# Query blocks in order 0, 1, 3, 2, dense blocks' activations ahead of the one-hot rows, and weight halves formed a pair ahead

## Chip, cores and metric

The kernel runs on one core of a Trainium2 chip. The metric is the device time of one execution in microseconds, as a median over runs. The engines of the core each run their own list of instructions in order: TensorE (PE, matmuls), VectorE (DVE), ScalarE (ACT), GpSimd (POOL) and SyncE (SP, which here issues most transfers). They wait for one another by semaphores.

## What is computed

A layer norm of x (2048 tokens of width 512) feeds two branches, and the output is x plus both:

```python
# attention: 32 heads of 16, one shared key and value head
scores = einsum("bhqd,bkd->bhqk", xn @ wq, xn @ wk) * 16 ** -0.5
att    = (softmax(scores) @ (xn @ wv)) @ wo
...
# product-key experts: 8 chunks of 4 heads, 64 x 64 = 4096 experts
s1, s2 = q1 @ k1.T, q2 @ k2.T                  # 64 scores each, per token and head
# the two best of each, the two best of their four sums, softmax g over these two
act = gelu(einsum("nd,nhkd->nhk", xn, u[top_e]))
out = einsum("nhk,nhk,nhkd->nd", g, act, v[top_e])
```

The inputs are float32. Each token picks 32 heads times 2 experts = 64 rows of u and of v.

## The kernel before, in words

**Attention.** The queries stand in four blocks of 512 tokens. A unit is one query block and four heads, 32 units in all, listed in `units` (L293). Each unit passes over 16 key tiles, two of them to a step, so the main loop has 256 steps `d`, with `i = 2 * d` (`att_steps`, L1040). A step issues 4 score matmuls (`scores`, L318), 16 matmuls of the previous step's probabilities with the values (`pv`, L332), and 4 more score matmuls; ACT takes the exponentials (L321, four of 128 x 1024 to a step). When two units are done, their sums and rows go through DRAM (`pair_*`, L363 to L382) to the normalised `on` tiles. Four `on` tiles are one query block, which is then multiplied with `wo` in four groups of 4 matmuls (`block_out`, L423, output `pwo`). `wo` lies in two of the 12 tiles of 512 KB that the gathers use also (`load_wo`, L387; `lent`).

**Experts by gathers.** Token groups 0 and 1 (8 tiles of 128 tokens) fetch their rows: a slot is one tile, head and choice pair of 128 experts, 512 slots in all. POOL starts an indirect DMA of 512 KB (`g`, L883), DVE forms the dot with xn (L895), four slots together pass small operations and a tanh on ACT (L904 to L918), and DVE adds the weighted rows to the tile's total `xa` (L930). A new gather may start when there is a free tile: the order is fixed as the gather of slot m + 12 after the add of slot m (m + 10 while `lent` is 2; `gathers`, L937).

**Experts as dense products.** Token groups 2 and 3 multiply with all 4096 experts in 32 blocks of 128 (`dense`, L648). Before this, the indices and gates of the group's 32 heads, held in `da` tiles (L631 to L641), are transposed on PE (`ptd`, L714) and spread: for each 16 tokens, 32 times (`q` loop, L744), DVE compares with a table of positions `io` (L725, L727), multiplies the gates in (L728), and PE multiplies the two one-hot operands of each token (`pg`, L752, 32 columns wide) to a 128 x 32 table of gates. ACT copies it (L757), and it goes to DRAM (`dg`) and comes back by block (`gy<-dg`, `fetch_gates`). Then for each block b, L791 to L861: load the u and v rows (`rw`, `fetch`), split each into a rounded half and the rest (`split`: ACT L687, DVE L688, into `wk` tiles), 12 matmuls with the group's xn (`pact`, L799), the gelu chain on ACT and DVE (`gy`, L821 to L828), a split of its result (`wd`, L835), and for each two blocks 24 matmuls to the four token tiles (`pout`, L783), each group added to the tile's total on DVE (`da`, L786).

**What sets the order.** Inside `tc.manual_schedule` nothing is reordered: each engine runs what the text issues, in that order. Each step takes the attention work and then `fill()` lets `score_thread` (L1001) run ahead to a linear target of estimated cost, so PE's fill is evenly laid over the steps: first the scores of group 0's 8 chunks, two chunks of group 1, then group 2 with its dense part, six chunks of group 1, then group 3 with its dense part. DVE's slot work goes by a rate `pos` per step (L1155: 2.1 slots, later 1.7, 2.5 in the one-hot rows or 1.4 in the blocks, by `dense_on`), and from step 192 on what is left is laid evenly over the remaining steps. `mid()` issues the DVE work in the middle of a step; `behind`, `store`, `on_act`, `LATER`, `LAST` and `LATER_ACT` put single operations off to the next step's DVE, SP or ACT part. `flush()` issues them at once.

**Sums of the branches.** For query blocks 0 to 2 the two branches meet through DRAM: whichever is done first is stored to `d_part`, and the other loads it (`fin`, one buffer), adds and stores the output (`load_fin` L418, `block_out`, `experts_out` L446). `att_steps` issues the `pwo` groups of a block in every second step from `i % 128 == 16` on. The DVE addition of the attention part to a loaded `fin` is L433, that of the experts' part L452. Block 3 is added straight to its experts' total by `last_out_a` and `last_out_b` (L396, L402).

Of the kernel before, what the change touches and what calls it, by code (L numbers as in the profile page):

```python
# [23 lines left out]
P = 128  # L24
S = 2048
D = 512
# [22 lines left out]
C_CUB = 0.044715 * C_IN  # L49
MOST = 4.0  # L50
# [4 lines left out]
def tile_kernel(ctx, tc, x, wq, wkv, wo, wqT, kT, uv, ub, vb, out):  # L55
# [17 lines left out]
    d_w = [dram.tile([P, KC, 2, 512], F32, name=f"dw{c}") for c in range(NC)]  # L73
    d_g = dram.tile([NB, P, 512], F32, name="dg")
# [218 lines left out]
    units = [(qb, hg) for qb in range(4) for hg in range(8)]  # L293
# [43 lines left out]
    def unit_tail(u):  # L337
# [4 lines left out]
        def spread():  # L342
            if half == 0:
                ot = late[0].tile([P, 512], F32, name="ot", tag="ot", bufs=1)
                OT[pp] = ot
                if pp == 15:
                    rs = late[0].tile([P, 512], F32, name="rsb", tag="on", bufs=4)
                    RB[pp] = rs
# [29 lines left out]
    def pair_tail(pp):  # L378
        rs = RB.pop(pp)
        on = late[0].tile([P, 512], F32, name="on", tag="on", bufs=4)  # L380
        nc.vector.tensor_mul(on, OT.pop(pp), rs)
        ON[pp] = on  # L382

    DONE_A, DONE_B, OUTS = {}, {}, []
# [17 lines left out]
    def last_out_b():  # L402
# [6 lines left out]
        for j in range(4):  # L409
            t = 12 + j  # L410
            nc.vector.tensor_add(ACC[t], ACC[t], PL[j])
            (nc.sync, nc.scalar)[j % 2].dma_start(out[t * P:(t + 1) * P, :], ACC[t])
# [3 lines left out]
    FIN = {}  # L416

    def load_fin(t):  # L418
        fin = late[0].tile([P, D], F32, name="fin", tag="fin", bufs=1)
        nc.sync.dma_start(fin, d_part[t])  # L420
        FIN[t] = fin

    def block_out(qb, j):  # L423
        t = 4 * qb + j
        p = xtile("pwo")
        for k in range(KC):
            nc.tensor.matmul(p, ON[4 * qb + k][:, j * P:(j + 1) * P], WO[k // 2][:, k % 2, :],  # L427
                             start=k == 0, stop=k == KC - 1)
        if t in FIN:
            fin = FIN.pop(t)  # L430

            def total():
                nc.vector.tensor_add(fin, fin, p)  # L433
                store(lambda: nc.sync.dma_start(out[t * P:(t + 1) * P, :], fin))

            behind(total)
        else:
            def keep():
                fin = late[0].tile([P, D], F32, name="fin", tag="fin", bufs=1)
                nc.scalar.copy(fin, p)  # L440
                store(lambda: nc.sync.dma_start(d_part[t], fin))

            on_act(keep)
        DONE_A[t] = True

    def experts_out(t):  # L446

        if t >= 12:
            return True
        if t in FIN:  # L450
            fin = FIN.pop(t)
            nc.vector.tensor_add(fin, fin, ACC[t])  # L452
            store(lambda: nc.sync.dma_start(out[t * P:(t + 1) * P, :], fin))
        elif t in DONE_A:
            load_fin(t)
            return False
        else:
            acc = ACC[t]
            store(lambda: nc.sync.dma_start(d_part[t], acc))
        DONE_B[t] = True  # L460
        return True
# [94 lines left out]
    DT = []  # L556
# [7 lines left out]
    def batch(ph, c, b):  # L564
# [52 lines left out]
        if c == 0:  # L617
            DT.clear()
            dense_tiles()
# [14 lines left out]
        def gates():  # L634
# [8 lines left out]
            stt(dgt[:, :, 1, w], gg, GS, gh, op0=OP.mult, op1=OP.subtract)  # L643

# [3 lines left out]
    def dense(DG, after):  # L648

        df1, df2, dgt = DT[:3]  # L650
# [12 lines left out]
        def gate_tile(b):  # L663
            if b not in gates:
                gy = late[0].tile([P, 2, 512], F32, name="gy", tag="gy", bufs=3)
                gates[b] = gy
            return gates[b]

        def fetch_gates(b):
            if b < NB and b not in fetched:  # L670
                if formed[0] < b - 2:
# [3 lines left out]
                nc.sync.dma_start(gate_tile(b)[:, 0, :], d_g[b])  # L675
                fetched.add(b)

        splits, halved = {}, set()

        def split(b):  # L680
            if b < NB:
                if b not in raws:
                    run(STORES)
                rw = raws.pop(b)
                us, vs = wk_tile(), wk_tile()
                for i, w in enumerate((us, vs)):
                    nc.scalar.copy(w[:, 0, :], rw[:, i, :])  # L687
                    behind(lambda w=w, i=i: nc.vector.tensor_tensor(out=w[:, 1, :], in0=rw[:, i, :], in1=w[:, 0, :],  # L688
                                                                    op=OP.subtract))
                behind(lambda: halved.add(b))  # L690
                splits[b] = us, vs
# [11 lines left out]
        io = kt(F16, (P, P, TB))  # L703
# [4 lines left out]
        tr = kt(F16, (P, 3, 512))  # L708
        for n, src in enumerate((df1, df2, dgt)):
            if n == 2:  # L710
                yield None
            p = xtile("ptd")
            for j in range(GT):
                nc.tensor.transpose(p[:, j * P:(j + 1) * P], src[:, j].rearrange("p r s -> p (r s)"), ident)  # L714
            nc.scalar.copy(tr[:, n, :], p)
            yield 0.45
        dense_on[0] = 2
# [3 lines left out]
        def onehot(q):  # L721
            if q < NQ:
# [3 lines left out]
                ob = kt(F16, (P, NB, TB))  # L726
# [4 lines left out]
        def first_gates():  # L731

            fetch_gates(0)
            fetch_gates(1)
            for j in range(2):
                da = big.tile([P, 2, D], F32, name="da", tag="da", bufs=2)
                for i in range(2):
                    t = GT * DG + 2 * j + i
                    nc.sync.dma_start(da[:, i, :], x[t * P:(t + 1) * P, :])
                    ACC[t] = da[:, i, :]  # L740

        onehot(0)
        onehot(1)
        for q in range(NQ):  # L744
# [10 lines left out]
            def copies(pv_=pv_, st=st, ql=ql, t0=t0):  # L755
                for hb in range(2):
                    nc.scalar.copy(st[hb][:, :, ql * TB:(ql + 1) * TB], pv_[:, 16 * hb:16 * hb + 16, :])  # L757
                if ql == 3:
                    for hb in range(2):
                        store(lambda hb=hb: nc.sync.dma_start(  # L760
# [501 lines left out]
```

## Time and profile before

| | |
|---|---|
| median of 3 runs | 1995.04 us (1994.63, 1995.04, 2007.21) |
| the profiled execution, its own time | 2001.03 us |
| its span in the trace | 1999.3 us |
| PE busy | 1882.9 us, 94% |
| DVE busy | 1682.7 us, 84% |
| ACT busy | 1292.0 us, 65% |
| POOL busy | 570.8 us, 29% |
| DMA | 494.79 MB, 247 GB/s on average |

How to read it: a row of the windows view gives one stretch of the span, from and to in microseconds, its length, the busy time and number of instructions of each engine, the granted clock of PE as a share of full speed, and the busy share of the DMA engines. A row of the waits view gives engine and line that waited, what it waited for, the sum, how often, and the longest. A row of the timeline gives start, busy time, engine, line and what the instruction writes and reads; where the engine stood idle ahead of it, the idle time and its releaser stand in brackets. Busy times of neighbouring instructions on one engine overlap a little, so the price of one is the distance between two starts.

### The profile page before, as it was taken

How to read it: one execution, taken by the hardware profiler on the slowest of the kernel's cores; microseconds unless marked ns; L12 is line 12 of the kernel's file. 1: busy time of each engine (PE TensorE's matmuls, PEld its weight loads, DVE VectorE, ACT ScalarE, POOL GpSimd, SP SyncE). 2: the span in 40 equal slices, each digit the busy share in tenths (PEclk: the TensorE clock that was granted, in tenths of full speed). 3: DMA queues.
4: the chain of work that ended last, by engine and by line, in shares of the span. 5: the costliest groups of instructions: out<-in, count | busy, mean ns of one | idle time of the engine just before them, and what ended most of it. 6: DMA issues, size and time to landing. Idle time of an engine off the chain costs nothing.

```text
span 1999.3 us, 34729 instructions
## 1 busy us (share of the span) xinstructions
PE 1882.9 (94%) x10990; PEld 997.5 (50%) x10990; DVE 1682.7 (84%) x6713; ACT 1292.0 (65%) x1804; POOL 570.8 (29%) x542
## 2 busy tenths in 40 slices
PE   6869999999998998999999999999899789999997
PEld 4534444555554444555555455555445345555552
DVE  7537888999998786999999779999999668999993
ACT  3236666655556785787877565555568567788873
POOL 2202232222222232333444222222223333333320
PEclk9989999999997998999999999999979899999999
DMA  7847878977664878888889877777568877888762
GB/s 272 301 185 235 276 272 272 331 275 248 218 212 140 229 221 271 264 269 269 284 297 328 286 253 261 268 238 225 176 169 234 276 245 263 268 277 257 263 211 63
DMA packets 239882, 494.79 MB, mean 247 GB/s; under 512 B 93380, under 2 KB 93380, under 8 KB 239692
## 3 DMA queue, kind: packets, MB, share of 16 engines
q0 software_dynamic: 73728, 268.47, 40.5%
q1 hardware_dynamic: 163960, 222.44, 34.0%
q10 hardware_dynamic: 2004, 1.61, 0.3%
q8 instruction: 88, 1.44, 0.3%
q14 instruction: 102, 0.84, 0.1%
HBM read 429.51 MB, written 57.64 MB: 244 GB/s over the span
## 4 chain that ended last, share of the span: by engine, by line
PE 63%; DVE 20%; DMA 5%; issue 2%; ACT 2%; SPq 1%; DVEq 0%; ACTq 0%
PE pv L332 18%; PE sc L318 12%; PE psc L532 10%; PE pout L783 8%; PE pact L799 8%; DVE i L547 5%; DVE xa L930 4%; DVE m L545 3%; DVE g L895 3%; PE pg L752 3%; PE pw L487 2%; PE pwo L427 1%; DMA dg<-gst 1%; ACT pt L321 1%; DMA fin<-dpart 1%
## 5 line engine op out<-in xcount | busy, mean ns | idle before, releaser
L321 ACT ACTIVATE pt<-sc 128x1024 f32<-128x1024 f32 x1024 | 993.0, 1025 | 471.1 <-PE sc L318 424.6
L883 POOL DMA_INDIRECT g<-in_uv_dram,idx x512 | 554.0, 1082 | 1358.4 <-DVE xa L930 697.4
L332 PE MATMUL pv<-pt,vaug 128*32 128x512 f32 x4096 | 524.1, 631 | 0.0
L318 PE MATMUL sc<-qa,kaug 64*128 64x512 f32 x2048 | 389.1, 454 | 14.4 <-ACT pt L321 13.5
L532 PE MATMUL psc<-wk,xt 128*128 128x512 f32 x1536 | 388.2, 400 | 5.3 <-DMA xt<-dxt 3.2
L930 DVE SCALAR_TENSOR_TENSOR xa<-g,w,xa 128x512 f32<-128x512 f32 x512 | 370.6, 745 | 0.0
L895 DVE CUSTOM_DVE_ANT_0 g<-g,xa 128x512 f32<-128x512 f32 x512 | 336.1, 681 | 3.0 <-DMA g<-in_uv_dram,idx 3.0
L532 PEld LDWEIGHTS psc<-wk,xt 128*128 128x128 f32 x1536 | 277.8, 188 | 108.7 <-issue 38.5
L318 PEld LDWEIGHTS sc<-qa,kaug 64*128 64x128 f32 x2048 | 157.6, 187 | 338.2 <-ACT pt L321 203.5
L332 PEld LDWEIGHTS pv<-pt,vaug 128*32 128x32 f32 x4096 | 110.7, 113 | 263.4 <-issue 261.7
L799 PE MATMUL pact<-xt,wk 128*128 128x512 f32 x768 | 198.7, 404 | 14.6 <-DVE fin L433 6.3
L547 DVE FIND_INDEX8 i<-m,psc 128x8 uint32<-128x64 f32 x1024 | 206.4, 221 | 0.0
L783 PE MATMUL pout<-wk,wd 128*128 128x512 f32 x768 | 195.7, 402 | 8.7 <-DVE wd L835 4.7
L799 PEld LDWEIGHTS pact<-xt,wk 128*128 128x128 f32 x768 | 141.1, 190 | 65.4 <-issue 17.7
L783 PEld LDWEIGHTS pout<-wk,wd 128*128 128x128 f32 x768 | 140.6, 188 | 56.7 <-DVE wd L835 6.0
L545 DVE MAX8 m<-psc 128x8 f32<-128x64 f32 x1024 | 146.0, 214 | 22.2 <-PE psc L532 19.8
L786 DVE TENSOR_TENSOR da<-da,pout 128x512 f32<-128x512 f32 x128 | 82.7, 679 | 8.2 <-PE pout L783 7.9
L918 DVE SCALAR_TENSOR_TENSOR w<-gth,ga 128x4 f32<-128x4 f32 x128 | 20.2, 158 | 79.9 <-ACT gth L911 79.4
L688 DVE TENSOR_TENSOR wk<-rw,wk 128x512 fp32r<-128x512 f32 x128 | 84.8, 682 | 0.1
L725 DVE TENSOR_TENSOR oh<-oh 128x2048 f16<-128x2048 f16 x64 | 78.0, 1219 | 7.1 <-PE pg L752 7.1
L752 PE MATMUL pg<-oh 128*128 128x32 f16 x1024 | 73.4, 246 | 8.1 <-DVE oh L728 8.1
L687 ACT CAST wk<-rw 128x512 fp32r<-128x512 f32 x128 | 73.6, 628 | 9.0 <-DMA rw<-in_ub_dram 6.7
(150 smaller groups left out, 1341.8 us busy)
## 6 DMA issues: line engine op xcount, KB each, us to landing
wk<-dw SPq DMA_DIRECT2D x96, 512.0 KB
wqt<-in_wqT_dram SPq DMA_DIRECT2D x32, 512.0 KB
dw<-wk SPq DMA_DIRECT2D x32, 512.0 KB
rw<-in_ub_dram SPq DMA_DIRECT2D x64, 256.0 KB
rw<-in_vb_dram SPq DMA_DIRECT2D x64, 256.0 KB
dg<-gst SPq DMA_DIRECT2D x32, 512.0 KB
gy<-dg SPq DMA_DIRECT2D x64, 256.0 KB
qa<-dqh SPq DMA_DIRECT2D x128, 64.0 KB
```

Of the source, the lines that this page charges most:

```text
L318: nc.tensor.matmul(p[:, b, :], kaug[o:o + 64, kc * P:(kc + 1) * P], QA[u][o:o + 64, i, :], start=True, stop=True)
L321: nc.scalar.activation(pt, p, AF.Exp, scale=SCALE)
L332: nc.tensor.matmul(PV[u][32 * j:32 * j + 32, :], vaug[:, kc, :], pt[:, b, :], start=kc == 0, stop=kc == 15)
L532: nc.tensor.matmul(p, XT[g][k][:, a, j * P:(j + 1) * P], WC[n_][k][:, bb, :], start=n == 0, stop=n == 11)
L545: nc.vector.max(m8[:, jb, s, :], p[:, s * E:(s + 1) * E])
L547: nc.vector.max_index(i8[:, jb, s, :], m8[:, jb, s, :], p[:, s * E:(s + 1) * E])
L752: nc.tensor.matmul(p[:, i * NB:(i + 1) * NB], oa[:, :, i], ob[:, :, i], start=True, stop=True)
L783: nc.tensor.matmul(p, wd[:, a, j * P:(j + 1) * P], vs[:, c, :], start=n == 0, stop=n == 5)
L799: nc.tensor.matmul(p, us[:, a, k * P:(k + 1) * P], XT[DG][k][:, c, :], start=n == 0, stop=n == 11)
L883: nc.gpsimd.indirect_dma_start(out=gt, out_offset=None, in_=uv, in_offset=bass.IndirectOffsetOnAxis(ap=IDX[ph, c, ti][:, s:s + 1], axis=0))
L895: nc.vector.tensor_tensor_reduce(u, u, XN[TPH * ph + ti], scale=1.0, scalar=0.0, op0=OP.mult, op1=OP.add, accum_out=a[:, i:i + 1])
L930: nc.vector.scalar_tensor_tensor(acc, v, w[:, i:i + 1], acc, op0=OP.mult, op1=OP.add)
```

## The change

1. **Order of blocks.** The units go through query blocks 0, 1, 3, 2 (`QB`). Block 2 is now the last, whose attention meets the experts' totals at the end; its totals, finished by then, are stored to `d_part` and loaded back as `FT` three steps before the end of attention (`load_last`).
2. **Sums.** `fin`, `load_fin` and the additions through it are gone. `block_out` adds each `pwo` group by one DVE operation to the token tile's total itself (`xa` or `da`), which must be loaded by then (`LIVE`). `experts_out` only stores. The groups of block 0 and block 3 are issued between dense blocks 2, 3 and 4, or from `i % 128 >= 56` on, those of block 1 every second step as before. `wo` stays in its two gather tiles until `i % 128 == 64` (before: 30), but for `256 < i < 384`.
3. **First blocks early.** The dense generator starts ahead of the last chunk's four tiles: it loads the u and v rows of blocks 0 and 1 and splits the u halves while that chunk is scored. The 12 `pact` matmuls of block 0 and its chain up to (tanh + 1) times the product (`first(0)`) are issued ahead of the first transposes, those of block 1 after the first one-hot row. Only the multiplication by the gates is left for later. The table `io` comes by DMA from `d_io`, written in the prologue by one ACT copy and one store, in place of a POOL copy.
4. **Splits ahead.** The splits of blocks 0 to 3 are issued during the last eight of the 32 one-hot rows (before: of 0 and 1, in the last two rows, of 2 and 3 with the first blocks), the u halves of 2 and 3 ahead of their v halves. The three small one-hot operands lie in a ring of one tile. The last `gst` tile is stored in three parts: gates of blocks 0 to 2 first, then 3 to 15, then 16 to 31. The totals of the group (`da`) are loaded at block 2.
5. **Slots.** From the last but one one-hot row until block 4, and from the last chunk's third tile until the transposes are done (`dense_on` 3), the slot rate is 0 (before: 1.4 or 1.7) and at most one addition is issued in a step. Dots are no longer asked for beyond the gathers that were issued.
6. The `on` tiles have 5 buffers (before 4).

Both programs have 11928 PE and 7263 DVE instructions; ACT has 3 fewer, POOL 2 fewer and SP 11 fewer (1215 for 1226).

The diff, cut to its core:

```diff
+    d_io = dram.tile([P, P, 16], F16, name="dio")
...
+        io = gtile(F16, (P, P, 16))
+        nc.scalar.copy(io, iota_h[:, :, None].to_broadcast([P, P, 16]))
+        nc.sync.dma_start(d_io, io)
...
-    units = [(qb, hg) for qb in range(4) for hg in range(8)]
+    QB = (0, 1, 3, 2)
+    units = [(qb, hg) for qb in QB for hg in range(8)]
...
+    def block_out():
+        m, j = PWO.pop(0)
+        t = GT * QB[m] + j
...
-        if t in FIN:
...
+        acc = ACC[t]
+        behind(lambda: nc.vector.tensor_add(acc, acc, p))
...
+        store(lambda: nc.sync.dma_start(d_part[t] if last else out[t * P:(t + 1) * P, :], acc))
...
     def dense(DG, after):
...
+        def half_split(b, i):
+            rw, w = raws[b], wk_tile()
+            nc.scalar.copy(w[:, 0, :], rw[:, i, :])
+            behind(lambda: nc.vector.tensor_tensor(out=w[:, 1, :], in0=rw[:, i, :], in1=w[:, 0, :], op=OP.subtract))
+            return w
...
-        nc.gpsimd.tensor_copy(io, iota_h[:, :, None].to_broadcast([P, P, TB]))
+
         fetch(0)
         fetch(1)
-        yield None
...
+        yield 0.0
+        early = []
+        on_act(lambda: early.extend(half_split(b, 0) for b in range(2)))
+        yield 0.0
...
+        def first(b):
+            p = xtile("pact")
+            for k in activations(b, early[b], p):
+                if k < KC - 1:
+                    yield 3 * UNIT
+            g, y = gate_rows(b), hh[:, b, :]
+            nc.scalar.activation(y, p, AF.Square, scale=C_CUB ** 0.5)
+            nc.scalar.copy(g, p)
+            nc.vector.scalar_tensor_tensor(y, y, C_IN, p, op0=OP.add, op1=OP.mult)
+
+            def go():
+                nc.scalar.activation(y, y, AF.Tanh)
+                behind(lambda: nc.vector.scalar_tensor_tensor(y, y, 1.0, g, op0=OP.add, op1=OP.mult))
...
+        nc.sync.dma_start(io, d_io)
...
+        yield from first(0)
+        for n in range(2):
+            spread(n)
             yield 0.45
+        while not gated_all:
+            yield None
+        spread(2)
+        yield 0.45
...
+        obs = kt(F16, (P, 3, NB, TB))
         onehot(0)
+        yield from first(1)
         onehot(1)
         for q in range(NQ):
...
-            if q >= NQ - 2:
-                dense_on[0] = 1
-                later_split(q - NQ + 2)
+            if q in (NQ - 8, NQ - 5):
+                later_split((NQ - 8, NQ - 5).index(q))
+            if q == NQ - 3:
+                on_act(lambda: halves.__setitem__(2, half_split(2, 0)))
+            if q == NQ - 2:
+                dense_on[0] = 3
+                on_act(lambda: halves.__setitem__(3, half_split(3, 0)))
+                later_split(2)
+            if q == NQ - 1:
+                later_split(3)
...
+            def scaled(y=y, g=g):
+                multiplied[0] += 1
+                stt(g, g, 1.0 / GS, y, op0=OP.mult, op1=OP.mult)
...
+            if b == 4:
+                dense_on[0] = 1
+            if b in (2, 3) and out_ready():
+                block_out()
+                yield 3.6
...
     def score_thread():
...
+            if ph >= NSP and c == NC - 1:
+                dn = dense(ph, n + 1 if n + 1 < len(SEQ) else None)
+                yield next(dn)
             for ti in range(TPH):
+                if dn and ti == 1:
+                    yield next(dn)
+                if dn and ti == 2:
+                    dense_on[0] = 3
...
     def att_steps(d, mid, fill):
...
-        if out_now:
-            block_out(qb, j)
+        if out_ready() and (i % 128 >= HOLD and PWO[0][0] != 1 or i % 4 == 0 and PWO[0][0] == 1):
+            block_out()
             spent[0] += 3.6
...
+        if i == STEPS - 6:
+            load_last()
-        if i >= 128 and i % 128 == 30:
+        if i >= 128 and i % 128 == (30 if 256 < i < 384 else HOLD + 8):
             lent[0] = 0
...
-                pos += 2.1 if len(IDX) < NC * TPH else (1.7, 2.5, 1.4)[dense_on[0]]
+                pos += 2.1 if len(IDX) < NC * TPH else (1.7, 2.5, 1.4, 0.0)[dense_on[0]]
             else:
-                pos += max(0.0, NSL - pos) / max(half - 4 - d, 1)
+                pos += max(0.0, NSL - pos) / max(half - 4 - d, 1) if dense_on[0] < 3 else 0.0
...
+                if dense_on[0] == 3:
+                    sums = min(sums, 1)
```

More of the change, by code (lines that the diff above doesn't have):

```diff
@@ L423, in block_out @@
-    def block_out(qb, j):
-        t = 4 * qb + j
+    LIVE = set(range(GT))
+    PWO = []
+    def block_out():
+        m, j = PWO.pop(0)
+        t = GT * QB[m] + j
         p = xtile("pwo")
         for k in range(KC):
-            nc.tensor.matmul(p, ON[4 * qb + k][:, j * P:(j + 1) * P], WO[k // 2][:, k % 2, :],
+            nc.tensor.matmul(p, ON[4 * m + k][:, j * P:(j + 1) * P], WO[k // 2][:, k % 2, :],
                              start=k == 0, stop=k == KC - 1)
-        if t in FIN:
[L430 to L443, printed above, removed]
+        assert t in LIVE
+        acc = ACC[t]
+        behind(lambda: nc.vector.tensor_add(acc, acc, p))
@@ L444, in block_out, with out_ready @@
         DONE_A[t] = True
+    def out_ready():
+        return PWO and GT * QB[PWO[0][0]] + PWO[0][1] in LIVE
     def experts_out(t):
[L448 to L459, printed above, removed]
@@ L683, in split @@
                     run(STORES)
[L684 to L689, printed above, removed]
+                us = None if b < 2 else halves.pop(b) if b in halves else half_split(b, 0)
+                splits[b] = us, half_split(b, 1)
                 behind(lambda: halved.add(b))
-                splits[b] = us, vs
+                raws.pop(b)
         def later_split(b):
@@ L1013, in score_thread @@
             if ph >= NSP and c == NC - 1:
[L1014 removed]
+                yield from dn
                 dense_on[0] = 0
```

214 lines of the change are left out of this document (120 added, 94 removed).

## The prediction

> **What bounds the kernel now.** I read the page first, for the bound and the chain, then the windows view over the stretches around the two dense groups, then the waits inside them, then the timeline for prices.
>
> ```profile
> span 1999.3 us, 34729 instructions
> PE 1882.9 (94%) x10990; PEld 997.5 (50%) x10990; DVE 1682.7 (84%) x6713; ACT 1292.0 (65%) x1804; POOL 570.8 (29%) x542
> ...
> PE 63%; DVE 20%; DMA 5%; issue 2%; ACT 2%; SPq 1%; DVEq 0%; ACTq 0%
> ```
>
> PE is busy for 94% of the span and carries 63% of the chain; DVE is second with 84% and 20%. Both programs have the same number of PE and of DVE instructions, so a gain must come from time in which PE stands, or runs on a lowered clock, and a loss from places where DVE has more to do than PE. The rows of the stretches:
>
> ```profile
> core 0: us, PE busy (x) PEld busy (x) DVE busy (x) ACT busy (x) POOL busy (x), PEclk, DMA share, GB/s
> 597.00:621.00 24.00, 16.49 (x118) 7.26 (x116) 23.34 (x119) 14.31 (x20) 8.36 (x7) 0.90 0.56 178
> 621.00:657.20 36.20, 36.20 (x285) 17.24 (x283) 30.56 (x64) 24.79 (x42) 5.88 (x5) 0.74 0.41 125
> 657.20:741.50 84.30, 83.37 (x692) 41.81 (x690) 64.19 (x135) 68.50 (x110) 23.75 (x21) 0.98 0.84 227
> 741.50:800.00 58.50, 47.10 (x234) 22.24 (x238) 40.68 (x95) 36.96 (x54) 18.26 (x18) 0.85 0.83 271
> 1439.00:1463.50 24.50, 12.93 (x95) 6.81 (x94) 23.85 (x127) 10.24 (x15) 4.24 (x4) 0.78 0.40 140
> 1463.50:1558.00 94.50, 91.79 (x825) 47.91 (x824) 88.59 (x186) 75.27 (x127) 26.67 (x22) 0.88 0.78 209
> 1558.00:1648.00 90.00, 75.42 (x369) 33.45 (x367) 57.68 (x139) 53.04 (x76) 30.63 (x27) 0.89 0.82 268
> 1648.00:1960.00 312.00, 310.36 (x1758) 170.63 (x1760) 282.22 (x646) 244.11 (x346) 106.25 (x96) 1.00 0.76 247
> ```
>
> I call lost PE time the idle time plus the busy time times what the clock lacks. First group: index work and transposes (597 to 621) 24.00 - 16.49 + 16.49 x 0.10 = 9.2 us; one-hot rows (621 to 741.5) 36.20 x 0.26 + 0.93 + 83.37 x 0.02 = 12.0; first blocks (741.5 to 800) 11.4 + 47.10 x 0.15 = 18.5. Second group: 11.6 + 12.93 x 0.22 = 14.4; 2.7 + 91.79 x 0.12 = 13.7; 14.6 + 75.42 x 0.11 = 22.9. Together 90.7 us. The last row is the tail, the second group's blocks: PE loses 1.6 us in 312, while DVE is idle for 29.8. What PE waits for in those places:
>
> ```profile
> PE ptd L714 <- DVE da L631: 9.4, 2, 8.7
> PE pg L752 <- DVE oh L728: 8.1, 6, 2.7
> ...
> PE pact L799 <- DVE fin L433: 6.3, 1, 6.3
> ...
> PE pact L799 <- ACT wk L687: 5.0, 1, 5.0
> ```
>
> These are of the whole span. Inside 741.5 to 791, and then inside 1558 to 1648:
>
> ```profile
> PE pact L799 <- DVE wk L688: 3.3, 1, 3.3
> ...
> ACT wk L687 <- DMA rw<-in_ub_dram: 6.7, 1, 6.7
> ```
>
> ```profile
> PE pout L783 <- DVE fin L433: 3.6, 1, 3.6
> ...
> PE pwo L427 <- DVE fin L433: 1.4, 1, 1.4
> ...
> DVE fin L433 <- DMA fin<-dpart: 25.3, 3, 12.9
> ```
>
> So four things stop PE: DVE's index work ahead of the transposes, DVE's one-hot operands, splits that wait for late u and v rows, and, after the second group's one-hot rows, DVE standing 25.3 us behind three loads of `fin`.
>
> Prices of DVE work, by the distance of starts:
>
> ```profile
> 1700.29 0.68 DVE L825 SCALAR_TENSOR_TENSOR gy<-gy,pact 128x512 f32<-128x512 f32 x1
> 1700.89 0.68 DVE L895 CUSTOM_DVE_ANT_0 g<-g,xa 128x512 f32<-128x512 f32 x1
> ...
> 1701.50 0.68 DVE L895 CUSTOM_DVE_ANT_0 g<-g,xa 128x512 f32<-128x512 f32 x1
> ...
> 1703.45 1.40 DVE L930 SCALAR_TENSOR_TENSOR xa<-g,w,xa 128x512 f32<-128x512 f32 x2
> 1704.78 0.68 DVE L822 SCALAR_TENSOR_TENSOR gy<-gy,pact 128x512 f32<-128x512 f32 x1
> ```
>
> ```profile
> 1481.81 0.16 DVE L906 TENSOR_TENSOR ga<-act,gg 128x4 f32<-128x4 f32 x1
> 1481.89 1.22 DVE L725 TENSOR_TENSOR oh<-oh 128x2048 f16<-128x2048 f16 x1
> ...
> 1483.81 1.22 DVE L725 TENSOR_TENSOR oh<-oh 128x2048 f16<-128x2048 f16 x1
> ```
>
> A 512-wide operation takes 0.60, a dot 0.61, an addition 0.67 (two in 1.33), a small one 0.08; with four small ones to four slots a slot takes 1.35 us. A one-hot row takes 1.92.
>
> **The change, part by part.** The places of the work are counted in the written order of both programs, by attention step.
>
> *A. First transition and one-hot rows.* 24 `pact` matmuls (blocks 0 and 1) now stand among the transposes. By the first of the page's rows below, 198.7 / 768 = 0.26 us each, they are 6.2 us that PE has to do where it waited.
>
> ```profile
> L799 PE MATMUL pact<-xt,wk 128*128 128x512 f32 x768 | 198.7, 404 | 14.6 <-DVE fin L433 6.3
> L783 PE MATMUL pout<-wk,wd 128*128 128x512 f32 x768 | 195.7, 402 | 8.7 <-DVE wd L835 4.7
> ```
>
> Also 8 dots and 7 additions (10 us of DVE) that stood among the index work are issued later. I take 7 us off the 9.2. In the one-hot rows up to step 82 the change takes 16 `pwo` matmuls out of PE and adds five u and v subtractions (3.0 us) to DVE; both then have about 88 to 91 us of work over sixteen steps, so DVE still holds PE at times: 2 us off the 12.0. Ends: 0 and -21.2. A = -9.
>
> *B. First blocks.* The waits for `wk` (5.0, 3.3) and for the u rows (6.7 on ACT) end in splits of blocks 0 and 1 that are asked for in the last two rows. Issued eight and five rows before the end, at about 6 us a row, they have 30 us for a load. Late next is the gates' store and load (`dg`, `gy`), covered by block 2's 12 matmuls and the block-0 output groups placed there. -16 of 18.5; ends -18.5 and, if those gates come as late as the rows did, -8.
>
> *C. Second transition.* The same 6.2 us of matmuls stand against 11.6 idle. But only one `pg` group instead of two comes before the next attention step, and DVE has its backlog of slots behind it: -4; ends 0 and -11.6.
>
> *D. Second one-hot rows.* DVE gets more in the sixteen steps after the transposes: 35 dots for 31, 34 additions for 29, two one-hot rows more, in all 9.8 us by the prices above; 89 of 94.5 us were already busy. 5.9 us are slack, of which I count 2.3 as usable (the rest ended in waits on tanh that stay): +7.5. By the written order two dots there stand only 3.1 and 3.8 us of DVE work behind the addition that lets their gather start:
>
> ```profile
> 1563.70 1.56 POOL L883 DMA_INDIRECT g<-in_uv_dram,idx  x1 [0.30 <-issue]
> 1565.57 1.05 POOL L883 DMA_INDIRECT g<-in_uv_dram,idx  x1 [0.31 <-issue]
> ```
>
> ```profile
> 1569.48 0.70 DVE L895 CUSTOM_DVE_ANT_0 g<-g,xa 128x512 f32<-128x512 f32 x1 [0.53 <-DMA g<-in_uv_dram,idx]
> ...
> 1571.63 0.69 DVE L895 CUSTOM_DVE_ANT_0 g<-g,xa 128x512 f32<-128x512 f32 x1 [1.44 <-DMA g<-in_uv_dram,idx]
> ```
>
> Gathers issued at 1563.70 and 1565.57 held the dots of 1569.48 and 1571.63: 5.8 and 6.1 us from start to use. Two such waits: +2.5. D = +10; ends +4 and +16.
>
> *E. `fin`.* Without the loads DVE no longer stands 25.3 us, and PE's 6.3, 3.6 and 1.4 go, with the low clock behind them: -19 of 22.9; ends -15 and -22.9 (the rate 0 leaves DVE with 20 us of work there against PE's 47, so nothing else can hold PE but `wd`).
>
> *F. The tail.* What DVE doesn't do in the blocks' start it does later: the last 44 steps of attention (from step 208) hold 141 dots and 138 additions, before 103 and 103. 38 dots, 35 additions, ten groups of small operations more, two `fin` additions and four subtractions fewer and six `gy` operations more make +44 us by the prices above. DVE was busy 282.2 of 312 us; with 326 it passes PE's 310, which stays as it is (30 matmuls of `pact` and `pout` fewer, 8 of `pwo` more, 3.6 us to four by the code's own estimate: -7.8 + 7.2). So DVE sets the tail. Its idle time there was
>
> ```profile
> DVE w L918 <- ACT gth L911: 11.2, 13, 1.9
> DVE gy L828 <- ACT gy L842: 7.5, 10, 1.9
> ```
>
> and smaller. Lower end: all idle time closes, 326 - 312 = +14. Upper end: all 29.8 us stay, +44, and gathers add. In steps 210 to 222 `wo` still holds two of the 12 tiles, and of three or four dots to a step several stand only 1.9 to 5.8 us behind their gather's release; at 6.1 us of latency these waits sum to 27 us, at 4.5 to about 8: +71 at the very end. I take half of the idle time that the waits above leave (+4) and 12 us of gather waits, since DVE that is behind anyway gives a gather more time than its own work: F = 14 + 4 + 12 = +30.
>
> The latency may be weighed against the Trainium skill, page "DMA: Bandwidth & Descriptors", section "Anatomy of one DMA — SWDGE (gpsimd) path": a fixed 2.0 us plus the bytes over 436 GB/s. For 512 KB an estimate from it is 3.2 us, where the two rows above show 5.8 and 6.1; the trace disagrees. By the page's figure the waits would nearly vanish, F would be about +19 and the forecast 11 us lower.
>
> *Elsewhere.* The store and two loads of `d_io` (512 KB each) and the later `wo` lie beside PE work; in the prologue an ACT copy may add up to 2 us. Block 1's `pwo` additions meet `xa` tiles loaded at least a step before; if one is late, DVE has there 15 us less work than PE in ten steps, so nothing. `FT` comes back three steps ahead of its use. Adding to `da` instead of `fin` is one DVE operation either way. 0, ends -2 and +5.
>
> **Sum.** -9 - 16 - 4 + 10 - 19 + 30 = -8 us against the profiled execution's own 2001.0, which stands 6.0 above the median of 1995.04; so against the median 1987.
>
> **The rivals.**
> *Faster: the tail absorbs.* If DVE, once behind, never waits (tanh and gathers are then long done), F is +14, and D its lower end +4: -9 - 16 - 4 + 4 - 19 + 14 = -30, 1965. For it: an engine that is behind meets finished inputs; the longest wait named above is 1.9 us. Against: those waits recur with every block, since tanh stands behind exponentials on ACT that need PE, which DVE holds.
> *Slower: gathers set the tail.* Each slot's addition releases the gather whose dot comes ten slots on. If the latency is 6.1 us or more and DVE's idle time also stays, F is +71 and the sum +33: 2028. It decides (above 2015) once F passes +58, a mean wait of some 0.2 us at each of the 141 dots beside the old idle time. For it: 5.8 and 6.1 above at a DMA share of 0.82. Against: only 13 steps have short leads.
> *The early blocks don't cover.* If the transposes still wait for DVE and the first blocks for gates instead of splits (A and C 0, B -8), the sum is -8 + 10 - 19 + 30 = +13, 2008: the change would do half of what it says. For it: DVE's index work is as long as before. Against: 10 us of slots are gone from that place.
> *The clock.* The stretch 621 to 657 was busy for 36.20 of 36.20 us at a clock of 0.74, so here the clock stayed low under a busy PE, and A keeps most of its 12.0. The Trainium skill, page "TensorE: Matmul & The Clock Gate", Part 1, says that about 3.4 us of sustained work give full clock back; the row disagrees. If the low clock is only the echo of the idle time ahead of it, closing that idle time gives A some -18 where I have -9: 1978.
>
> **How the numbers follow.** Forecast 0.42, its own range 1975 to 2003; the tail absorbs 0.24; gathers set the tail 0.16; no cover 0.10; the clock 0.08. Less than 1% (20 us: below 1975 or above 2015) cannot be told from no change. Faster by over 1%: most of the second (0.20), part of the clock (0.03) and of the forecast's low side (0.09): 0.32. Slower: 0.12 of the third, 0.03 of the fourth, 0.05 for D and F both at their ends in the forecast: 0.20. Same 0.48. The range goes from 1958 (below the first rival by the spread of A to C) to 2022, leaving about 0.1 on each side.
>
> **What would show it.** A: the `ptd` wait of 8.7 gone, clock above 0.9 in the rows. B, E: no `wk` and no `fin` wait; PE idle under 4 us between one-hot rows and block 5. D: DVE above 95% busy in the second rows. F: the stretch from step 208 to the end of attention longer than 312 us, with DVE near 95%, PE waiting on DVE, and dots waiting on gathers early in it. If that stretch is 312 us again I was wrong on F; if the stretches before it are not 30 to 45 us shorter, on A to E.

## The result: 1.6% slower, and the profile after

The changed kernel takes 2027.29 us (median of 4, 2021.49 to 2033.16); the kernel before, measured with it, 2000.47 us (median of 4, 1994.63 to 2007.21). The ratio is 1.0155, with a 95% interval of 1.0125 to 1.0185: slower. The forecast was 1987 with a range from 1958 to 2022, so the measured time lies 5 us above the range. The profiled execution took 2021.49 us, its span is 2019.8 us, 20.5 us more than before.

The page of the changed kernel:

```profile
span 2019.8 us, 34706 instructions
PE 1888.2 (93%) x10990; PEld 1001.1 (50%) x10990; DVE 1679.9 (83%) x6713; ACT 1293.9 (64%) x1801; POOL 571.2 (28%) x540
...
PE 48%; DVE 30%; DMA 8%; issue 4%; ACT 2%; POOL 1%; SPq 0%; ACTq 0%; DVEq 0%; POOLq 0%
...
L969 DVE CUSTOM_DVE_ANT_0 g<-g,xa 128x512 f32<-128x512 f32 x512 | 336.1, 685 | 35.3 <-DMA g<-in_uv_dram,idx 35.3
```

The engines are about as busy as before, but the chain has moved: PE's share fell from 63% to 48%, DVE rose from 20% to 30%, DMA from 5% to 8%. The last row is new in kind: the dots waited 35.3 us for their gathers (3.0 before).

The same steps as in the prediction's table of stretches (the times are those of the changed kernel; the last row is the tail, before 312 us from 1648 on):

```profile
core 0: us, PE busy (x) PEld busy (x) DVE busy (x) ACT busy (x) POOL busy (x), PEclk, DMA share, GB/s
595.20:622.00 26.80, 22.04 (x143) 11.53 (x142) 17.95 (x98) 16.65 (x24) 0.93 (x1) 0.87 0.23 69
622.00:649.40 27.40, 27.40 (x267) 14.89 (x266) 26.99 (x59) 24.38 (x42) 2.36 (x2) 0.94 0.53 138
649.40:741.30 91.90, 87.29 (x707) 44.04 (x706) 72.04 (x144) 72.56 (x117) 24.59 (x20) 0.91 0.86 242
741.30:783.00 41.70, 41.70 (x231) 21.74 (x230) 22.92 (x45) 32.17 (x43) 2.08 (x2) 1.00 0.36 102
1424.40:1442.50 18.10, 15.66 (x100) 8.58 (x99) 11.82 (x77) 11.56 (x16) 0.94 (x1) 0.91 0.13 39
1442.50:1537.60 95.10, 89.06 (x795) 46.57 (x794) 88.67 (x191) 75.83 (x127) 25.23 (x23) 0.89 0.67 192
1537.60:1616.50 78.90, 72.31 (x413) 35.49 (x412) 48.81 (x99) 54.32 (x77) 15.22 (x12) 0.89 0.74 227
1616.50:1976.00 359.50, 321.68 (x1721) 172.39 (x1720) 321.97 (x778) 242.39 (x347) 153.55 (x134) 0.96 0.80 266
```

The first blocks (fourth row) run without an idle microsecond at full clock, where PE lost 18.5 us before. The second transition and the second blocks are shorter too. All of it is given back in the last row: DVE does 322 us of work there for 282, and PE, busy for 310 of 312 before, now idles 38 us. What the two engines wait for in that row:

```profile
DVE g L969 <- DMA g<-in_uv_dram,idx: 30.4, 23, 2.8
DVE da L846 <- PE pout L843: 4.2, 3, 2.6
```

```profile
PE pout L843 <- DVE gy L886: 18.8, 7, 5.2
PE pout L843 <- DVE da L436: 6.0, 2, 3.1
PE pout L843 <- DVE wd L901: 4.8, 2, 2.6
```

DVE stands behind gathers in its own queue, and PE's `pout` waits for what is queued behind the standing dot. Nearly all of DVE's standing lies in steps 208 to 222; the chain of waits there, in order of time:

```profile
1651.85 1.13 POOL g L957
...
1653.30 5.46 DMA g<-in_uv_dram,idx
...
1658.90 0.69 DVE g L969
1659.60 0.66 DVE xa L1004
...
1660.53 1.13 POOL g L957
...
1662.05 6.88 DMA g<-in_uv_dram,idx
...
1668.95 0.69 DVE g L969
```

The chain runs from gather to gather: a dot (`g`) waits for its rows, the addition (`xa`) behind it frees a tile, POOL starts the next gathers, and a later dot waits for one of these. POOL starts one gather after the other, so a POOL row here is the gather ahead of the one whose landing the DMA row shows. The two gathers that were waited for started on POOL at 1653.30 and 1662.05 and were used at 1658.90 and 1668.95, 5.6 and 6.9 us later. Over all 23 waits of the last row of the table, pairing gathers and dots in their order, that time is 4.5 to 7.3 us, in the middle 5.8. In the kernel before three dots waited for a gather, 5.8 to 8.6 us after its start: the gathers did not become slower.

The waits end when `wo` gives back its two tiles. In 1616.5 to 1747 and then in 1747 to 1976 they are

```profile
DVE g L969 <- DMA g<-in_uv_dram,idx: 29.8, 20, 2.8
```

```profile
DVE g L969 <- DMA g<-in_uv_dram,idx: 0.5, 3, 0.2
```

and the tail asks for 3.2 dots a step in both parts. With ten tiles a dot comes 6.4 us (median) after its gather's start, with twelve 10.2 us.

For the comparison of kernels I take the start of each attention step from PE's rows, and the lengths between them in microseconds. The table counts steps from the first that has `pv` matmuls, 150 to 153 us into the span, so its step 207 is `d` = 208 of the code. "Dots" are those of the written order from `d` = 208 on, the tail.

| kernel | to 60 | 60-100 | 100-180 | 180-201 | 201-207 | 207-254 | rest | dots |
|---|---|---|---|---|---|---|---|---|
| before | 432.2 | 289.0 | 559.7 | 145.6 | 62.8 | 333.5 | 25.1 | 103 |
| changed | 429.9 | 272.4 | 562.8 | 151.0 | 42.2 | 383.1 | 27.8 | 141 |
| e1 | 445.9 | 283.4 | 569.4 | 144.9 | 45.7 | 333.0 | 27.0 | 119 |
| e2 | 436.5 | 270.8 | 563.5 | 150.0 | 42.2 | 392.8 | 27.8 | 141 |
| e3 | 434.1 | 284.6 | 558.3 | 147.2 | 52.9 | 331.3 | 26.9 | 109 |
| e4 | 435.3 | 284.4 | 562.9 | 146.9 | 52.3 | 331.9 | 27.1 | 109 |
| e5 | 441.6 | 271.4 | 561.6 | 148.2 | 41.7 | 360.3 | 27.7 | 141 |
| e6 | 436.1 | 278.5 | 562.7 | 165.9 | 42.0 | 388.9 | 26.7 | 141 |
| e7 | 440.3 | 269.2 | 567.3 | 141.9 | 44.8 | 336.5 | 26.8 | 123 |
| e8 | 434.9 | 292.2 | 563.1 | 144.1 | 51.8 | 333.2 | 25.6 | 103 |
| e9 | 438.1 | 272.2 | 567.6 | 144.2 | 44.0 | 366.2 | 26.6 | 132 |
| e10 | 434.2 | 268.8 | 577.9 | 143.5 | 45.8 | 331.2 | 27.0 | 116 |
| e11 | 433.9 | 271.4 | 565.5 | 145.9 | 48.5 | 331.1 | 26.5 | 103 |

The column to step 60 differs by up to 12 us between kernels whose text is the same that far (429.9 in the changed kernel, 441.6 in e5), so it tells spread between executions, and the columns behind it are to be compared. Each row is one profiled execution.

### The profile page after: what moved, and what is told of

It is laid out like the page before. It is cut to its first block, busy times and chain, and to the rows that moved or that the text cites. A ratio compares the mean times of both kernels' runs of the same rounds, so it can differ in the third digit from the quotient of the medians.

```text
span 2019.8 us, 34706 instructions
## 1 busy us (share of the span) xinstructions
PE 1888.2 (93%) x10990; PEld 1001.1 (50%) x10990; DVE 1679.9 (83%) x6713; ACT 1293.9 (64%) x1801; POOL 571.2 (28%) x540
## 4 chain that ended last, share of the span: by engine, by line
PE 48%; DVE 30%; DMA 8%; issue 4%; ACT 2%; POOL 1%; SPq 0%; ACTq 0%; DVEq 0%; POOLq 0%
PE pv L339 14%; PE sc L325 9%; PE psc L527 9%; DVE xa L1004 6%; DVE g L969 5%; PE pout L843 5%; PE pact L719 5%; DVE i L542 5%; DMA g<-in_uv_dram,idx 4%; DVE m L540 3%; PE pg L801 2%; PE pw L482 2%; PE pwo L432 1%; ACT pt L328 1%; DVE oh L767 1%
## 5 line engine op out<-in xcount | busy, mean ns | idle before, releaser
L339 PE MATMUL pv<-pt,vaug 128*32 128x512 f32 x4096 | 518.2, 624 | 0.0
L325 PE MATMUL sc<-qa,kaug 64*128 64x512 f32 x2048 | 388.5, 454 | 15.3 <-ACT pt L328 14.4
L969 DVE CUSTOM_DVE_ANT_0 g<-g,xa 128x512 f32<-128x512 f32 x512 | 336.1, 685 | 35.3 <-DMA g<-in_uv_dram,idx 35.3
L843 PE MATMUL pout<-wk,wd 128*128 128x512 f32 x768 | 205.5, 416 | 36.0 <-DVE gy L886 18.8
L843 PEld LDWEIGHTS pout<-wk,wd 128*128 128x128 f32 x768 | 146.1, 196 | 88.3 <-DVE gy L886 22.1
L719 PEld LDWEIGHTS pact<-xt,wk 128*128 128x128 f32 x768 | 139.2, 188 | 54.5 <-issue 19.4
L801 PEld LDWEIGHTS <-oh 128*128 128x128 f16 x1024 | 69.3, 164 | 20.1 <-issue 11.0
```

Of the source, the lines that this page charges most:

```text
L325: nc.tensor.matmul(p[:, b, :], kaug[o:o + 64, kc * P:(kc + 1) * P], QA[u][o:o + 64, i, :], start=True, stop=True)
L339: nc.tensor.matmul(PV[u][32 * j:32 * j + 32, :], vaug[:, kc, :], pt[:, b, :], start=kc == 0, stop=kc == 15)
L719: nc.tensor.matmul(p, us[:, a, k * P:(k + 1) * P], XT[DG][k][:, c, :], start=n == 0, stop=n == 11)
L801: nc.tensor.matmul(p[:, i * NB:(i + 1) * NB], oa[:, :, i], ob[:, :, i], start=True, stop=True)
L843: nc.tensor.matmul(p, wd[0][:, a, j * P:(j + 1) * P], vs[:, c, :], start=n == 0, stop=n == 5)
L969: nc.vector.tensor_tensor_reduce(u, u, XN[TPH * ph + ti], scale=1.0, scalar=0.0, op0=OP.mult, op1=OP.add, accum_out=a[:, i:i + 1])
```

## The experiments

Two theories stood at first. S: the zero slot rate puts 38 slots off into the tail, and DVE becomes its bound. R: the two gather tiles that `wo` holds until step 224 let gathers start too late. (In the rates of the edits below, chosen by `dense_on`, 1.4 belongs to the one-hot rows and 2.5 to the blocks; the description of the kernel before has the two the other way round.)

**e1: more slots in the middle.**

```diff
-(1.7, 2.5, 1.4, 0.0)[dense_on[0]]
+(1.95, 2.5, 1.7, 0.0)[dense_on[0]]
```

> The changed kernel with the slot rate raised where the first dense blocks and the six chunks after them run (1.4 to 1.7 and 1.7 to 1.95). 119 dots instead of 141 are left for the tail (from step 208), DVE work there about 291 us against PE's 305. Theory S (slots put off make DVE the bound of the tail): 25 to 35 us faster than the changed kernel, about 1995, DVE waits on gathers under 12 us. Rival R (the two gather tiles that wo holds until step 224 are the cause): waits on gathers stay near 25 us, 5 to 10 us faster, about 2018. If the middle has no DVE slack to take 22 slots: no gain, the loss moves there.

Measured: 2007.23 us (1.0043 of before, 1.0019 to 1.0068), 20 us faster than the changed kernel; the waits on gathers fell from 35.3 to 7.2 us and the tail to 333.0, as long as before. S holds in the tail, though 20 us are less than the 25 to 35 that it expected. Steps 60 to 180 cost 17.6 us more than in the changed kernel, 11.0 of them before step 100, where the raise from 1.4 to 1.7 fell on one-hot rows in which DVE was full already (26.99 of 27.40 us in the changed kernel's first rows).

**e2: `wo` back early.**

```diff
-if out_ready() and (i % 128 >= HOLD and ...
+if out_ready() and (i % 128 >= (HOLD if i < 384 else 28) and ...
...
-i % 128 == (30 if 256 < i < 384 else HOLD + 8)
+i % 128 == (30 if 256 < i < 384 else HOLD + 8 if i < 384 else 36)
```

> The changed kernel with the pwo groups of the last quarter issued from i % 128 >= 28 (for 56) and the two wo tiles returned at 36 (for 64). Theory R: DVE's waits on gathers fall from 35 to under 12 us and the time by 20 to 25 us, about 2004. Theory S: the tail keeps 137 dots, DVE stays the bound, waits shorten but the time falls by at most 10 us, about 2019.

Measured: 2038.49 us (1.0228, 1.0180 to 1.0277), the tail 392.8, 9.7 longer. The waits on gathers of the whole run are

```profile
DVE g L969 <- DMA g<-in_uv_dram,idx: 42.1, 29, 5.8
```

and went on to step 250. R's cure failed, and S's price was missed as well, since it expected a gain of up to 10. It is not a clean test of R. The earlier `pwo` groups push block 4 back, so by the written order the zero rate lasts two steps longer and 141 slots fall on 42 steps (3.36 a step) in place of 44 (3.2). At that rate gathers are late with 12 tiles too; in the changed kernel, at 3.2, they are late with ten and not with twelve. So the number of tiles and the slots asked for in each step both set the waits.

**e3: slots go on.**

```diff
-(1.7, 2.5, 1.4, 0.0)[dense_on[0]]
+(1.7, 2.5, 1.4, 1.4)[dense_on[0]]
...
-pos += max(0.0, NSL - pos) / max(half - 4 - d, 1) if dense_on[0] < 3 else 0.0
+pos += max(0.0, NSL - pos) / max(half - 4 - d, 1)
...
-sums = min(sums, 1)
+pass
```

> The changed kernel without the zero slot rate (1.4 in its place) and without the limit of one addition a step; wo is held as long as in the changed kernel. 109 dots in the tail (before: 103). Theory S: the tail falls back to the length of before, 50 us less, while the blocks' starts lose 5 to 15 of what they gained: about 1985 to 1990. Theory R: gathers still wait with ten tiles, the fall is under 20 us, above 2007. Rival Z (the zero rate pays for the gains at the blocks' starts): the tail falls by 50 but the starts lose 30 or more: about 2005.

Measured: 1989.78 us (0.9951, 0.9927 to 0.9976), 37 us faster than the changed kernel: the tail is 331.3 again. It also shows what the zero rate had bought: 12.2 us in steps 60 to 100 and 10.7 in 201 to 207, 22.9 for a price of 51.8 in the tail. That is between the 5 to 15 of S and the 30 of Z. Steps 100 to 201 were 8.3 us shorter as well; no run shows why.

**e4: both edits of e2 and e3.**

> Both edits of e2 and e3 together. Theory S alone: the same time as e3 within 4 us. Theory R as a part beside S: 5 to 15 us faster than e3. If the pwo groups earlier in the last quarter delay the first blocks: slower than e3 by up to 5 us.

Measured: 1988.57 us (0.9952, 0.9925 to 0.9978). The same as e3: with 109 slots in the tail (2.5 a step), how long `wo` holds its tiles is of no account.

**e5: the tail without gathers.**

```diff
+        if m >= NSL - 141:
+            UV[m] = kept[0]
+            if len(kept) < 2:
+                kept.append(gtile())
+            return
...
-        nc.vector.tensor_tensor_reduce(u, u, XN[TPH * ph + ti], ...
+        o = kept[1][:, :D] if m >= NSL - 141 else u
+        nc.vector.tensor_tensor_reduce(o, u, XN[TPH * ph + ti], ...
```

> The changed kernel without the last 141 gathers: the dots and additions of the tail all read one tile that is fetched already, so POOL and its DMA queue have nothing to do there, while DVE has the same operations. What it leaves out: the last 141 fetched rows, so the experts' part of the first two token groups is other data. It prices the two parts of the tail's loss. If waits on gathers are the larger part: the tail (step 207 to 254) falls by 30 or more of the 50 us it lost, to about 15 to 20 over before, the time to about 1993. If DVE's work itself is: it falls by under 10 us, above 2015.

Measured: 2002.57 us (1.0037, 1.0013 to 1.0061); the tail is 360.3, which lies between the two expectations. Steps 208 to 252 of this run, without a gather:

```profile
1623.70:1960.50 336.80, 313.74 (x1723) 167.31 (x1722) 327.43 (x778) 242.08 (x347) 0.00 (x0) 0.98 0.23 75
```

DVE is busy for 327 of 337 us, 97%: without any gather its own work sets the tail. It stood for 9.4 us, of which 4.3 for PE's `pout`. So the 49.6 us split into 22.8 (383.1 - 360.3) for gathers and 26.8 (360.3 - 333.5) for DVE's work.

**e6: block 0 not early.**

```diff
-        yield from first(0)
         for n in range(2):
...
         spread(2)
         yield 0.45
+        yield from first(0)
```

> The changed kernel with the 12 pact matmuls of block 0 and its chain issued after the third transposes, not ahead of the first ones. If they cover DVE's index work as the prediction has it (A 7 us, C 4 us): 8 to 14 us slower than the changed kernel, about 2037, and PE waits at ptd grow by as much. If the DVE chain is late either way: within 4 us of the changed kernel.

Measured: 2053.77 us (1.0281, 1.0230 to 1.0332), 26 us slower than the changed kernel. Steps 60 to 100 are 6.1 us longer, 180 to 201 even 14.9, in the tail another 5.8. The wait at the second transposes, 2.4 us in the changed kernel, is

```profile
PE ptd L744 <- DVE da L627: 9.8, 1, 9.8
```

So early matmuls do cover the index chain, and at the second group they are worth more than I had put down: the run is outside both of its expectations.

**e7: more slots only between the dense groups.**

```diff
 pos += 2.1 if len(IDX) < NC * TPH else (1.7, 2.5, 1.4, 0.0)[dense_on[0]]
+if d > 91 and dense_on[0] < 2:
+    pos += 0.24
```

> The changed kernel with 0.24 slots a step more from step 92 to the second dense group only (the raise of e1 also reached the steps ahead of step 60, which cost 13 us there). 123 dots are left for the tail, the zero rates stay. Theory S: the tail is as long as before (e1 with 119 dots showed that), DVE has 614 us of work against PE's 629 in the middle, so little is lost there: 40 to 48 us faster than the changed kernel, about 1981, about 1% faster than before. If DVE becomes the bound of the middle: 10 to 25 us of that are lost there.

Measured: 1981.50 us (0.9908, 0.9874 to 0.9943), 46 us faster than the changed kernel and 0.9% faster than before. The tail is 336.5; steps 100 to 180 cost 4.5 us more. The expectation says that e1's raise cost 13 us ahead of step 60. That is not shown: kernels with the unchanged text there took 429.9 to 441.6, e7 itself 440.3, and e1, with 7 slots more by then, 445.9.

**e8: the kernel before without the loads of `fin`.**

```diff
-        nc.sync.dma_start(fin, d_part[t])
...
-                nc.vector.tensor_add(fin, fin, p)
+                nc.vector.tensor_copy(fin, p)
...
-            nc.vector.tensor_add(fin, fin, ACC[t])
+            nc.vector.tensor_copy(fin, ACC[t])
```

> The kernel before without the loads of fin (fin takes a copy in place of the sum, so the other branch's part is missing for the tiles of the first three query blocks). It prices the fin waits alone. The prediction's step E says 15 to 23 us faster than before, about 1980. If the change's gain there came from the zero slot rate: under 12 us.

Measured: 1996.59 us (0.9970, 0.9932 to 1.0008), no difference that the whole time can show. Steps 201 to 207 fell by 11.0 us, from 62.8 to 51.8, which is nearly e3's 52.9. So the fin waits are worth 11 us, under the 12 that the expectation names, and the other 10 of the changed kernel's 20.6 there come from the zero rate. A part stays open: the one buffer still held DVE 8.6 us until a store was through.

**e9, e10: half and more of e7's raise** (0.12 and 0.34 in place of 0.24).

> As e7 with half the raise, 0.12 slots a step: 132 dots are left for the tail, DVE work there 308 us against PE's 305. It places the point from which the tail pays: with 123 dots it was 3 us over before (e7), with 141 50 us. If the loss grows evenly past the point where DVE's work equals PE's: about 25 us over before in the tail, time about 2003. If gather waits set in suddenly once three slots a step are asked of ten tiles: 35 or more, about 2013. If the point is higher: under 10, about 1988.

> As e7 with a raise of 0.34: 116 dots are left for the tail, DVE has 626 us of work in steps 90 to 181 against PE's 629. If only the tail counts: the 3 us of e7 there go, about 1979. If a DVE as full as PE costs in the middle: 5 to 15 us slower than e7.

Measured: e9 2010.52 us (1.0028, 0.9998 to 1.0059), its tail 366.2, 32.7 over before; e10 1983.36 us (0.9914, 0.9883 to 0.9944), its tail 331.2, but steps 100 to 180 are 10.6 us longer than e7's. So the tail's length by dots is flat to 119 (331 to 334), 336.5 at 123, 366.2 at 132, 383.1 at 141. e9 lies between its two forms, nearer to the sudden one; its waits on gathers are 26.5 us, none of them behind the return of the two tiles. All runs with more than 109 dots had ten tiles until then, e2 apart, so these lengths hold for this ring. And in the middle a raise of 0.34 is too much: between steps 90 and 180 of e10, DVE was busy for 606.86 of 647.80 us beside PE's 628.83 (626 and 629 by the expectation's count).

**e11: the zero rate at the first group only**, with e7's raise.

```diff
-(1.7, 2.5, 1.4, 0.0)[dense_on[0]]
+(1.7, 2.5, 1.4, 0.0 if d < 128 else 1.4)[dense_on[0]]
...
-pos += max(0.0, NSL - pos) / max(half - 4 - d, 1) if dense_on[0] < 3 else 0.0
+pos += max(0.0, NSL - pos) / max(half - 4 - d, 1)
...
-if dense_on[0] == 3:
+if dense_on[0] == 3 and d < 128:
```

> As e7, but with the zero rate and the limit on additions only at the first dense group; at the second 1.4 slots a step go on. 103 dots in the tail. The zero rate gained some 10 us in steps 201 to 207 (e3 against the changed kernel); if that holds, this is 7 to 10 us slower than e7 (its tail 3 us shorter), about 1989; if the second group's start does not need it, 1979.

Measured: 1980.80 us (0.9895, 0.9818 to 0.9972). Against e7, steps 180 to 207 are 7.7 us longer and the tail 5.4 shorter: even. The second group's start gains from the zero rate only what the tail pays for it. Steps 208 to 252 of this run:

```profile
1622.70:1930.30 307.60, 306.32 (x1723) 166.21 (x1722) 273.76 (x631) 239.94 (x337) 108.62 (x97) 1.00 0.75 249
```

PE is the bound again, at full clock. e7, e10 and e11 are about 1% faster than the kernel before; e3 and e4 are 0.5% faster.

## Why the prediction was wrong, step by step

The prediction's own measure, lost PE time (idle time plus busy time times what the clock lacks), gives for the rows of the changed kernel above: 26.80 - 22.04 + 22.04 x 0.13 = 7.6; 27.40 x 0.06 + 4.61 + 87.29 x 0.09 = 14.1; 0; 2.44 + 15.66 x 0.09 = 3.8; 6.04 + 89.06 x 0.11 = 15.8; 6.6 + 72.31 x 0.11 = 14.5; 37.8 + 321.68 x 0.04 = 50.7. The row of 14.5 holds the end of D and all of E; steps 201 to 207 alone are, before and in the changed kernel,

```profile
1577.90:1640.70 62.80, 48.74 (x222) 21.80 (x222) 36.42 (x86) 32.23 (x44) 20.88 (x18) 0.89 0.84 286
```

```profile
1566.70:1608.90 42.20, 41.88 (x224) 20.51 (x223) 18.63 (x31) 30.53 (x39) 4.29 (x4) 1.00 0.67 215
```

with 19.4 and 0.3 us lost, so that 3.5 and 14.2 fall to D.

| step | forecast | measured: lost PE time, changed less before |
|---|---|---|
| A, first transition and rows | -9 | 7.6 + 14.1 - 9.2 - 12.0 = +0.5 |
| B, first blocks | -16 | 0 - 18.5 = -18.5 |
| C, second transition | -4 | 3.8 - 14.4 = -10.6 |
| D, second rows | +10 | 15.8 + 14.2 - 13.7 - 3.5 = +12.8 |
| E, fin | -19 | 0.3 - 19.4 = -19.1 |
| F, the tail | +30 | 50.7 - 1.6 = +49.1 |
| sum | -8 | +14.2 |

Of the other 6.3 of the span's 20.5 us, 1.2 are PE's work in these stretches, and 5.1 lie outside them, 2.7 of these behind step 254. F missed by 19 us and A by 9.5; C, more than twice its forecast, hid 6.6 of that.

**F is the step that failed, by its size.** The mechanism was as forecast: DVE passes PE's work, PE waits for it, and dots with a short lead wait for gathers until step 222, while `wo` holds two tiles. I took 14 + 4 + 12 = 30; by step lengths F is 49.6. Of this, e5 shows 26.8 for DVE alone where I had 18. DVE's work was about right (322 us busy, forecast 326), but I let it close nearly all its idle time, and it still stood 9.4 us in e5. The sum behind the 326 does not add up as written: the operations listed, at their prices, make about 50 us and not 44, and there are six `gy` operations fewer (26 of each of three for 28), not more.

For the gathers I took 12 us and e5 shows 22.8. I had written down 27 for a latency of 6.1 us, which was near, and then discounted it, because a DVE that is behind gives a gather more time than its own work. It did not: the chain above shows that a gather starts behind an addition in DVE's own queue, so a late DVE starts it late too, and the median lead of 6.4 us left nothing over the 5.8 that the gathers took.

The rival "gathers set the tail" had 2028, and 2027 came, but the number agrees by luck: the rival needs F = +71, and says itself that it decides only past +58. Its mechanism did show, with a mean wait of 30.4 / 141 = 0.22 us at a dot, beside a DVE that was short of time without any gather.

The Trainium skill, page "DMA: Bandwidth & Descriptors", section "Anatomy of one DMA — SWDGE (gpsimd) path", was weighed there: fixed 2.0 us plus the bytes over 436 GB/s, an estimate of 3.2 us for 512 KB. The trace disagrees again (5.6 and 6.9 us in the rows above), and by the page's figure the waits that cost 22.8 us would hardly have been there, since the shortest lead in the tail is 4.4 us.

**A gave nothing, and C more than forecast: the wait stood at the other group.** I named the `ptd` wait of 8.7 us as A's sign. It belongs to C. The waits of before in 597 to 621 and in 1439 to 1463.5 are

```profile
PE ptd L714 <- DVE da L631: 0.7, 1, 0.7
```

```profile
PE ptd L714 <- DVE da L631: 8.7, 1, 8.7
```

The 7.5 us that PE stood in the first transition were 3.4 for exponentials, 3.4 for one-hot operands and 0.7 for `ptd`. In the changed kernel it stands there 4.7 us for `ptd`, so its lost time fell by 1.6 us, forecast 7. The early block does help (without it, in e6, steps 60 to 100 are 6.1 us longer), but against the kernel before little was there to cover. The one-hot rows lost 2.1 us more, forecast 2 less: DVE is busy for 26.99 of 27.40 us in the first of them, and at their end ACT held a split for late rows, with PE's scores waiting for the exponentials behind it. The waits of ACT and of PE in 627 to 741.3:

```profile
ACT wk L683 <- DMA rw<-in_ub_dram: 3.7, 1, 3.7
```

```profile
PE sc L325 <- ACT pt L328: 4.6, 8, 2.5
```

B counted about 6 us a row for these loads; by DVE's rows a one-hot row took 3.9 us before and 3.2 in the changed kernel, so they had less time. At the second transition the wait fell from 8.7 to 2.4 us and lost PE time by 10.6, with 24 early matmuls there (block 0's 12 alone are worth 14.9 in steps 180 to 201 by e6). Not all of it is theirs: PE stood 11.6 us there before, 2.4 in the changed kernel and 5.5 in e3, where the slots go on.

**B and E are right in size, and in part by luck.** Of the 16.6 us that steps 60 to 100 gained, 12.2 go when the slots go on (e3), and so do 10.7 of the 20.6 us (62.8 - 42.2) in E's steps; `fin` alone is worth 11.0 (e8), where E had 19. The prediction credited these gains to the splits and to `fin`; it named the rate 0 beside them (in A and E), but priced it only as a cost, in D and F. Why 25.3 us of DVE standing cost only 11 is not shown; PE's waits for `fin` in the whole kernel were 11.3 us (6.3, 3.6 and 1.4).

**D** is right to 3 us.

**The clock.** In the five steps behind the first transition the granted clock was 0.94 (622 to 649.4), before 0.74, and they took 27.4 us for 36.2. The idle time ahead of them was 4.8 us, before 7.5. Over the profiles of all thirteen kernels, the seven with 4.7 or 4.8 us of idle time there have 0.94 behind it, and the six with 6.1 to 11.0 us have 0.74 to 0.88. That fits the fourth rival, a low clock as an echo of the idle time ahead; no run changes the idle time alone. The Trainium skill, page "TensorE: Matmul & The Clock Gate", Part 1, has the low clock follow an idle window. That much the trace agrees on. But in the second one-hot rows it was 0.89, as before (0.88), with PE busy for 89.06 of 95.10 us and the idle time ahead down from 11.6 to 2.4 us: there closing the gap gave nothing.

## What to carry to other kernels

Work that is put off to clear a crowded stretch is paid where it lands, and the price there is not its duration: it is nothing as long as the engine has room, and more than its duration from the point where the engine becomes the bound. Here 22.9 us were bought for 51.8, and 18 of the slots put off, laid into a stretch with room (e7), cost 4.5 there and took 46.6 off the tail. Before slots are moved, compare the work of both engines in the stretch where they will land, and for a ring of buffers the lead of each transfer against its latency under load. Fewer buffers and more items asked for in each step both shorten the lead, and an engine that is late does not lengthen it when the release comes from its own queue.

## What the hardware showed beside this

Kernels with the same text that far differ by up to 12 us in the first 60 steps (429.9 in the changed kernel, 441.6 in e5), so a single profile of this kernel is to be compared by stretches and not by its span.
